# First layer's eleventh pair of steps nested, outer weight sums split between VectorE and POOL, and a transfer's room moved into finished weights

## The chip, the core and the metric

The kernel runs on one core of a Trainium2 chip. The metric is device time in microseconds, as the median of three executions: 848.37 us (848.19 to 848.67). One further execution was profiled: it took 848.57 us, and the program's span in its trace is 846.8 us, so 1.77 us of its time lie around the span. Every time below that is read from the trace belongs to that one execution, and is counted from the span's start.

## What is computed

An attention over 4 batches, 8 heads, 768 tokens and head size 64, in which a query sees only keys of the same 6-bit hash bucket, and then a two-layer network on the 3072 tokens:

```
scores = np.where(q_bucket == k_bucket, scale * q @ k.T, -1e9)
attn = softmax(scores);  x = (attn @ v) as (3072, 512)
h = x @ w_in                                 # (3072, 512) @ (512, 2048)
g = h * (1.0 / (1.0 + np.exp(-1.702 * h)))
return (g @ w_out).astype(np.float32)        # (3072, 2048) @ (2048, 512)
```

All of it is float32. The change is in the two layers of the network alone.

## The kernel before, in words

**Two layers as Strassen-like products.** Both layers use a seven-product scheme in place of eight (Winograd's form). One operand is cut into quarters `a11..a22`, and `sums_a` (lines 219 to 225) makes four sums of them, S1 to S4; the other is cut into `b11..b22`, and `sums_b` (L227 to L233) makes t1, d12, t2 and t4. The dictionaries `LEFT` and `RIGHT` say which quarter or sum each of the products 1 to 7 takes. A sum that is written `s3` stands in the place of `a21`, and `d12` in the place of `b12`.

**First layer.** The tokens come in three blocks of 1024 (`sb`), and for each block `MT` = 8 steps (`mt`) each make 128 columns of the hidden layer on either side of the cut: 24 steps, numbered n = 0 to 23. A step's seven products have two matrix instructions of 512 columns each (`product`, L895 to L900); float32 instructions appear as two records each in the trace. ScalarE applies the activation, POOL makes the second layer's outer sums of its result (`g_outer`), and each result goes to `g_dram` in device memory (`keep`, L902 to L910).

**Nested pairs.** Two steps 2t and 2t+1 can be run as one pair (`pair_of_steps`). There the products 2, 4 and 3 of the two steps together are again cut in quarters (`nest_w`, `nest_x`, `nested`, L969): seven instructions of 256 columns instead of eight, for each of the three. `NESTED` is the range of the pairs t that are run so: 1 to 9, which are the steps 2 to 19. Steps 0, 1 and 20 to 23 run through `hidden`. The pairs of even t hold their results in tiles of the pool `stage`, those of odd t in `twice`; the nested sums of weights are also in `twice`, and for t of 2 and 3 they hold a fourth tile, so that the quarter `x[2]` stays whole. A pair lays out part of its work for the other engines in `agenda`, in slots 1 to 17, of which the slots past 8 fall into the next pair or step.

**Second layer.** There are 21 outer products (`steps_out`, three token blocks times `OUTER` = 1, 2, 6, 7, 5, 3, 4), and each is again a seven-product scheme of 256 columns with four matrix instructions for each product (`product_of_halves`, L1217 to L1283, order of products 1, 2, 3, 6, 7, 5, 4). An outer product n needs three things: two transfers of 1 MB from `g_dram` (`fetch(n)`, L1176 to L1180; the first brings b11 and b12, the second b21 and b22), into one of two rooms (`raw_g[0]`, a tile of its own, for even n; `raw_g[1]`, in `s_in`, for odd n); the sums of what was fetched, by VectorE (`g_sums(n)`); and the sums inside its weights, by POOL (`inner_sums`, with places from the list `rooms`).

**The outer sums of the output weights.** The seven left operands `wqs` are four quarters of the converted `w_out_sb` and three sums over them, made by `sums_a` in two halves of columns, `low` and `high`, of four sums each. Before, all eight are VectorE's, and they are spread over steps 20 to 23 (`between` and `todo`).

**Order.** TensorE, VectorE, ScalarE and POOL run in the order in which the program gives its instructions. The queue of SyncE (SP), which issues the fetches and most of the stores, is ordered when the program is built, by the times that the builder estimates. It issues in that order, and an entry that waits holds back all entries behind it. ScalarE issues the conversion's loads and the nested pairs' direct stores on a queue of its own.

The conversion of `w_out` (lines 170 to 208, six VectorE instructions and one of ScalarE to a chunk) runs beside the first layer, the last of its 16 chunks at step 20.

Of the kernel before, what the change touches and what calls it, by code (L numbers as in the profile page):

```python
# [8 lines left out]
F32 = mybir.dt.float32  # L9
# [10 lines left out]
P = 128  # L20
# [18 lines left out]
def kernel(  # L39
# [17 lines left out]
    nc = tc.nc  # L57
# [178 lines left out]
    XT = 512  # L236
# [609 lines left out]
    def feed_forward(tag, late=()):  # L846
# [9 lines left out]
        with ExitStack() as fctx:  # L856
# [7 lines left out]
            twice_ctx = fctx.enter_context(ExitStack())  # L864
            twice = None
            MT = FC // 2
            NESTED = range(1, MT + 2)
            sets = [small_ctx.enter_context(tc.tile_pool(name=f"f1{tag}", bufs=1, space=PSUM, side="right"))]
# [14 lines left out]
            def staged_pair(name, second):  # L883

                held[name] = (twice if second else stage).tile([P, 2 * XT], F32, tag=name, name=name)
                return held[name]

            def staged(name, n):

                if n in (0, 2 * NESTED.stop) and (name, n) not in made:  # L890
                    made[name, n] = staged_pair(name, False)
                return held[name][:, n % 2 * XT : (n % 2 + 1) * XT]
# [40 lines left out]
            def nest_w(t):  # L933
                sums = {}
                m = slice(2 * t * P, (2 * t + 2) * P)
                for o in TWICE:
                    w = quarters_in(m)[LEFT[o]]
                    x = [w[:, k, i * P : (i + 1) * P] for i in range(2) for k in range(2)]
                    n = 3 if t < 2 else 4
                    new = w_out_sb[:, t - 2, 12:16, :] if (o, n) == (4, 4) else twice.tile([P, n, P], F32, name=f"w{o}{t}")  # L940
                    new = [new[:, i] for i in range(n)]
                    s3 = x[2] if n == 3 else new[3]
                    W[o, t] = [x[0], x[1], s3, x[3]] + new[0:3]
                    sums[o] = sums_a(nc.gpsimd, x[0], x[1], s3, x[3], *new[0:3], a21=x[2])
                return sums
# [57 lines left out]
            def plan(t, at, *fs, small=False):  # L1003
                agenda.setdefault(8 * t + at, ([], []))[0 if small else 1].extend(fs)
# [133 lines left out]
            def outer_sums(*args):  # L1138
                t = [x.tile([P, XT], F32, tag=f"t{i}", name=f"t{i}") for x in places_of_sums for i in (1, 2, 4)]
                for f in g_outer(*args, *(t or (args[2], args[5], args[4]))):  # L1140
                    for x in f:
# [9 lines left out]
                     for x in (xT[:, 3], s_room) for i in range(4)]  # L1151
            rooms[4:4] = [w_in_sb[:, :, F2 * i + mt * P : F2 * i + (mt + 1) * P] for mt in range(FC // 2) for i in range(2)]
            wholes = [xT[:, i, 4 * XT : 6 * XT] for i in range(4)] + [t_x[:, i].rearrange("p k t -> p (k t)") for i in range(2)]
# [18 lines left out]
            steps_out = [(sb, o) for sb in range(n1) for o in OUTER]  # L1172
            raw_g = [None, s_in[:, 0:2].rearrange("p i k f -> p (i k f)").rearrange("p (c t) -> p c t", t=XT)]

# [6 lines left out]

            g_tiles = {}

            def g_quarters(n):
                if n not in g_tiles:


                    g_tiles[n] = wholes[4:6] if n == 1 else [
                        (st2 if n % 2 else gp).tile([P, F4, TH], F32, tag=t, name=t + "ab"[n % 2]) for t in ("t1", "t2")]
                    g_tiles[n] = g_tiles[n] + [gp.tile([P, F4, TH], F32, tag="t4", name="t4g")]  # L1190
# [26 lines left out]
            def product_of_halves(n, acc, after):  # L1217
# [3 lines left out]
                m = wholes[n % len(wholes)]  # L1221
                u, v = (gp.tile([P, TH], F32, tag=x, name=x, bufs=2) for x in ("u", "v"))
                c11, c12, c21, c22 = (m[:, i] for i in range(4))
# [83 lines left out]
            twice = twice_ctx.enter_context(tc.tile_pool(name=f"tw{tag}", bufs=1, side="right"))  # L1307
            wop = fctx.enter_context(tc.tile_pool(name=f"wo{tag}", bufs=1))
            cv_ctx = fctx.enter_context(ExitStack())
# [11 lines left out]
                      for k, i in ((3, 0), (2, 0), (3, 0), (3, 1))]  # L1321
            spare += [s_in[:, 0:2, :, 0 : 2 * P], s_in[:, 2, :, 0:XT]]
# [12 lines left out]

# [13 lines left out]
            for t in NESTED:  # L1349
# [27 lines left out]
            for n in range(2 * NESTED.stop, 3 * MT):  # L1377
                sb, mt = divmod(n, MT)
                if n == 2 * NESTED.stop + 1:
                    assert not agenda  # L1380
                    inner_ctx.close()
                    twice_ctx.close()
# [12 lines left out]
            t_ctx.close()  # L1395
            stage_ctx.close()
            st2 = fctx.enter_context(tc.tile_pool(name=f"st2{tag}", bufs=1, side="right"))
# [110 lines left out]
```

## Time and profile before

| | |
|---|---|
| median of three runs | 848.37 us (848.19 to 848.67) |
| profiled execution: own time, span | 848.57 us, 846.8 us |
| TensorE busy, share of the span | 838.2 us, 99% |
| VectorE busy | 674.6 us, 80% |
| POOL busy | 366.3 us, 43% |
| ScalarE busy | 337.2 us, 40% |
| mean granted TensorE clock | 0.999 |
| attention | up to 308 us |
| first layer, TensorE | 308.44 to 586.3 us |
| second layer, TensorE | 586.3 to 840.3 us |

How to read the rows below: a row of the timeline has the start, the length (of several merged instructions, from the first start to the last end), the engine (SPq and ACTq are the queues in which SyncE and ScalarE issue transfers), the line, the operation, the tile written and the tiles read, the shape and a count; in brackets stands how long the engine was idle before, and what released it. A modelled end of a matrix instruction overlaps the next one's start, so the distance from start to start is its cost. A row of transfers gives their count, their size and the median time from issue to landing.

### The profile page before, as it was taken

The page shows a single profiled execution, that of the slowest core. Times are in us where ns is not written, and L with a number is a line of the kernel's source. Part 1 is how long each engine was busy: PE and PEld are TensorE (multiplying, and loading weights), DVE is VectorE, ACT ScalarE, POOL GpSimd, SP SyncE. Part 2 cuts the span into 40 slices and gives each one's busy share as a digit, 9 for nine tenths or more (in the row PEclk, how much of TensorE's full clock was granted, in tenths as well). Part 3 has the DMA queues.
Part 4 walks back from the last instruction along what each step waited for, and adds up shares of the span by engine and source line. Part 5 has one row for each costly group of instructions (what it writes and reads, how often), then busy time and mean ns, then how long its engine had stood idle before and what let it go on. Part 6 is the DMA issues. An engine that isn't in the chain of part 4 may idle for free.

```text
span 846.8 us, 14953 instructions
## 1 busy us (share of the span) xinstructions
PE 838.2 (99%) x5644; PEld 520.8 (62%) x5644; DVE 674.6 (80%) x1068; ACT 337.2 (40%) x552; POOL 366.3 (43%) x321
## 2 busy tenths in 40 slices
PE   9999999999999999999999999999999999999996
PEld 4544444444444444566666666545888888888885
DVE  6478888887888985788888788577998977796776
ACT  7766766767676634433444344433000000000000
POOL 5433443434344358996844486578655000000000
PEclk9999999999999999999999999999999999999999
DMA  8679766777763105445555545587754685467524
GB/s 143 120 154 167 163 131 142 146 150 148 155 156 95 49 2 174 150 158 215 216 196 198 210 174 224 198 298 257 264 192 156 195 254 192 155 201 248 194 106 101
DMA packets 165197, 144.92 MB, mean 171 GB/s; under 512 B 124224, under 2 KB 139712, under 8 KB 159872
## 3 DMA queue, kind: packets, MB, share of 16 engines
q1 hardware_dynamic: 154640, 112.11, 47.7%
q10 hardware_dynamic: 10480, 31.81, 11.3%
q8 instruction: 45, 0.74, 0.4%
q14 instruction: 32, 0.26, 0.1%
HBM read 79.69 MB, written 50.33 MB: 154 GB/s over the span
## 4 chain that ended last, share of the span: by engine, by line
PE 98%; POOL 1%; ACT 0%; issue 0%; DVE 0%; ACTq 0%; POOLq 0%
PE product L1228 30%; PE product L899 23%; PE s L547 15%; PE s L514 15%; PE small L969 6%; PE product L969 3%; PE s L496 2%; PE s L460 1%; PE s L569 1%; POOL above L339 0%; PE s L410 0%; POOL feat L337 0%; ACT c L914 0%; DVE v L917 0%; ACT size L198 0%
## 5 line engine op out<-in xcount | busy, mean ns | idle before, releaser
L484 ACT ACTIVATE e<-s 128x768 f32<-128x768 f32 x192 | 143.2, 812 | 49.2 <-PE s L514 43.9
L547 PE MATMUL s<-e,v 128*32 128x385 f32 x1536 | 130.9, 488 | 0.0
L525 POOL TENSOR_TENSOR t_x<-e 128x768 f32<-128x768 f32 x32 | 60.5, 1891 | 136.2 <-ACT e L484 126.1
L899 PE MATMUL product<-xT,w_in_sb 128*128 128x512 f32 x216 | 100.0, 593 | 0.1
L547 PEld LDWEIGHTS s<-e,v 128*32 128x32 f32 x1536 | 46.7, 109 | 79.3 <-issue 62.8
L899 PE MATMUL product<-t_x,s_in 128*128 128x512 f32 x192 | 89.5, 593 | 0.0
L514 PE MATMUL s<-s_in 32*128 32x384 f32 x912 | 87.8, 481 | 0.0
L525 POOL TENSOR_TENSOR t_x<-t_x,e 128x768 f32<-128x768 f32 x32 | 55.1, 1723 | 43.4 <-ACT e L484 42.0
L538 DVE TENSOR_TENSOR acc<-acc,e 128x768 f32<-128x768 f32 x63 | 70.1, 1113 | 2.3
L1264 ACT COPY u<-product 128x256 f32<-128x256 f32 x20 | 7.4, 372 | 158.4 <-PE product L1228 125.2
L899 PEld LDWEIGHTS product<-xT,w_in_sb 128*128 128x128 f32 x216 | 40.9, 190 | 35.8 <-issue 32.7
L514 PEld LDWEIGHTS s<-s_in 32*128 32x128 f32 x912 | 43.8, 185 | 23.4 <-issue 2.2
L899 PEld LDWEIGHTS product<-t_x,s_in 128*128 128x128 f32 x192 | 36.4, 190 | 29.9 <-issue 26.8
L514 PE MATMUL s<-own 32*128 32x384 f32 x432 | 44.3, 482 | 0.0
L465 DVE TENSOR_SCALAR f<-s,above,weight 128x384 bf16<-128x384 f32 x15 | 10.2, 678 | 39.1 <-PE s L569 33.9
L917 DVE TENSOR_TENSOR u<-product,u 128x256 f32<-128x256 f32 (+1 forms) x60 | 28.4, 486 | 15.5 <-PE product L969 12.9
L1228 PE MATMUL product<-raw_g,xT 128*128 128x256 f32 x152 | 35.1, 379 | 0.0
L535 DVE SCALAR_TENSOR_TENSOR acc<-t_x,e 128x768 f32<-128x768 f32 x31 | 29.3, 946 | 6.7 <-POOL t_x L525 3.6
L231 POOL TENSOR_TENSOR v<-c,v 128x1024 f32<-128x1024 f32 (+1 forms) x15 | 32.3, 2155 | 1.0
L230 POOL TENSOR_TENSOR u<-v,u 128x1024 f32<-128x1024 f32 (+1 forms) x11 | 23.8, 2166 | 20.6 <-ACT v L914 11.3
L917 DVE TENSOR_TENSOR v<-product,v 128x512 f32<-128x512 f32 x24 | 16.5, 689 | 20.0 <-PE product L899 20.0
L1228 PEld LDWEIGHTS product<-raw_g,xT 128*128 128x128 f32 x152 | 28.9, 190 | 3.9
(297 smaller groups left out, 1774.0 us busy)
## 6 DMA issues: line engine op xcount, KB each, us to landing
raw_g<-g_dram SPq DMA_DIRECT2D x20, 1024.0 KB, 5.1
s_in<-g_dram SPq DMA_DIRECT2D x20, 1024.0 KB, 5.0
g_dram<-c ACTq DMA_DIRECT2D x18, 512.0 KB, 2.8
raw<-in_moe_w_out_dram ACTq DMA_DIRECT2D x16, 512.0 KB, 3.7
raw<-in_moe_w_in_dram ACTq DMA_DIRECT2D x15, 512.0 KB, 3.8
s_in<-own SPq DMA_DIRECT2D x36, 192.0 KB, 4.0
v<-in_v_dram SPq DMA_DIRECT2D x16, 384.0 KB, 4.0
k<-in_k_dram SPq DMA_DIRECT2D x52, 96.0 KB, 3.0
```

Source lines behind the costliest of these rows:

```text
L230: return [lambda: eng.tensor_tensor(t1, b12, b11, op=Alu.subtract), lambda: eng.tensor_tensor(b12, b22, b12, op=Alu.subtract), lambda: eng ...
L231: lambda: eng.tensor_tensor(b12, b22, b12, op=Alu.subtract),
L484: nc.scalar.activation(es[c][:, kt, :, 0:HS], ps[:, :, 0:HS], Act.Exp, scale=1.0 / D**0.5)
L514: nc.tensor.matmul(ps[i][:, j, 0:HS], a[r0 : r0 + 32, keys], m[r0 : r0 + 32, cols], start=at == 0, stop=at == 2)
L525: nc.gpsimd.tensor_tensor(low_sum, low_sum if i else e[:, 0], e[:, i + 1], op=Alu.add)
L535: nc.vector.scalar_tensor_tensor(acc, terms[0], T * TINY, terms[1], op0=Alu.add, op1=Alu.add)
L538: nc.vector.tensor_tensor(acc, acc, terms[i + 1], op=Alu.add)
L547: nc.tensor.matmul(av[D * j + d : D * j + d + 32, :], vt[:, j, row, d : d + 32], es[c][:, t, j, :], start=(t == 0), stop=(t == T - 1))
L899: nc.tensor.matmul(ps, wq[LEFT[i]][:, kc, :], xq[RIGHT[i]][:, kc, :], start=(start and kc == 0), stop=(kc == K2 - 1), skip_group_check=not ...
L917: nc.vector.tensor_tensor(dst, x, y, op=Alu.add)
L969: nc.tensor.matmul(x, wq[LEFT[i]], xq[RIGHT[i]], start=start, stop=True, skip_group_check=True)
L1228: nc.tensor.matmul(ps, wq[LEFT[i]][:, c, :], gq[RIGHT[i]][:, c, :], start=(onto is None and c == 0), stop=(c == F4 - 1), skip_group_check= ...
```

## The change

- `NESTED` now ends with pair 10, so the steps 20 and 21 run as a nested pair too, and only 0, 1, 22 and 23 run through `hidden`. For t = 2 the nested weight sums now overwrite `x[2]`, and they have a pool of their own, `nest`.
- The eight outer sums of weights are dealt out: the four of `low` into slots 1, 5, 2, 3 of pair 10, three on POOL and one (the second) on VectorE; `high[0]` and `high[2]` on VectorE at the end of step 22 and within step 23, `high[1]` and `high[3]` on POOL behind step 23.
- `inner_sums(0)` stays at pair 9; `inner_sums(1)` is put at the end of step 22, ahead of that step's own outer sums of results, which are now written out at the start of step 23; `inner_sums(2)` comes at the end of step 23, with `g_sums(0)` in step 23 as well.
- `raw_g[0]` is no tile of its own any more but lies in the columns of `w_in_sb` that steps 0 to 3 of a token block use; `fetch(0)` stands ahead of step 22, `fetch(1)` within step 23. Eight new tiles (`more`) replace the rooms for inner sums that those columns had held.
- The tiles of `stage` are taken over for `wide` (VectorE's sums of fetched results, and the products' u and v), and `twice` stays open to the end of the first layer.

```diff
-            NESTED = range(1, MT + 2)
+            NESTED = range(1, MT + 3)
...
-                    n = 3 if t < 2 else 4
-                    new = w_out_sb[:, t - 2, 12:16, :] if (o, n) == (4, 4) else twice.tile([P, n, P], F32, name=f"w{o}{t}")
+                    n = 3 if t < 3 else 4
+                    new = w_out_sb[:, t - 2, 12:16, :] if (o, n) == (4, 4) else nest.tile([P, n, P], F32, name=f"w{o}{t}")
...
-            rooms[4:4] = [w_in_sb[:, :, F2 * i + mt * P : F2 * i + (mt + 1) * P] for mt in range(FC // 2) for i in range(2)]
+            rooms[4:4] = [w_in_sb[:, :, F2 * i + mt * P : F2 * i + (mt + 1) * P] for mt in range(4, FC // 2) for i in range(2)]
...
-            raw_g = [None, s_in[:, 0:2].rearrange("p i k f -> p (i k f)").rearrange("p (c t) -> p c t", t=XT)]
+            raw_g = [w_in_sb.rearrange("p c (i f) -> p (c i) f", i=2)[:, :, 0:XT], s_in[:, 0:2].rearrange("p i k f -> p (i k f)").rearrange("p (c t) -> p c t", t=XT)]
...
-            low, high = (sums_a(nc.vector, *(x[:, :, F4 * c : F4 * (c + 1), :] for x in wqs)) for c in range(2))
+            low, high = ([sums_a(eng, *(x[:, :, F4 * c : F4 * (c + 1), :] for x in wqs))[i] for i, eng in enumerate(engs)]
+                         for c, engs in enumerate(((nc.gpsimd, nc.vector, nc.gpsimd, nc.gpsimd),
+                                                   (nc.vector, nc.gpsimd, nc.vector, nc.gpsimd))))
             first = 2 * NESTED.stop
-            between = {first + 1: low[1:2], first + 2: high[:1], first + 3: high[2:3]}
-            todo[first] = todo.get(first, []) + low[:1]
-            todo[first + 1] = low[2:] + inner_sums(1)
-            todo[first + 2] = high[1:2]
-            todo[first + 3] = high[3:] + inner_sums(2)
+            todo[first] = high[:1] + inner_sums(1)
...
+                if t + 2 == NESTED.stop:
+                    plan(t, 5, *inner_sums(0))
                 if t + 1 == NESTED.stop:
-                    plan(t, 5, *inner_sums(0))
+                    for i, f in zip((1, 5, 2, 3), low):
+                        plan(t, i, f)
...
-                if n == 2 * NESTED.stop + 1:
+                between, end = [], []
+                if n == 2 * NESTED.stop:
+                    fetch(0)
+                else:
...
-                    raw_g[0] = gp.tile([P, FC // 2, XT], F32, name="raw_g")
+                    more = gp.tile([P, 8, F4, P], F32, name="rooms")
+                    rooms[8:8] = [more[:, i] for i in range(8)]
+                    wide += [stage.tile([P, 4, TH], F32, tag=x, name="wide") for x in ("u", "v", "c21", "c22")]
...
                     outer_sums(*heads.pop("sums"))
-                    fetch(0)
-                t = {3 * MT - 2: g_sums(0)[:1], 3 * MT - 1: g_sums(0)[1:]}.get(n, []) if n > 3 * MT - 3 else []
-                hidden(sb, mt, between.get(n, []) + ([lambda: fetch(1)] if n == 3 * MT - 1 else []), t + todo.pop(n, []))
+                    g = g_sums(0)
+                    between, end = [high[2], g[0], lambda: fetch(1)], g[1:] + inner_sums(2) + [high[1], high[3]]
+                hidden(sb, mt, between, todo.pop(n, []) + end)
```

More of the change, by code (lines that the diff above doesn't have):

```diff
@@ L865, in feed_forward @@
             twice = None
+            nest_ctx = fctx.enter_context(ExitStack())
+            nest = None
             MT = FC // 2
-            NESTED = range(1, MT + 2)
+            NESTED = range(1, MT + 3)
             sets = [small_ctx.enter_context(tc.tile_pool(name=f"f1{tag}", bufs=1, space=PSUM, side="right"))]
@@ L890, in staged @@
                 if n in (0, 2 * NESTED.stop) and (name, n) not in made:
-                    made[name, n] = staged_pair(name, False)
+                    made[name, n] = staged_pair(name, n > 0)
                 return held[name][:, n % 2 * XT : (n % 2 + 1) * XT]
@@ L1180, in fetch @@
                     loader[0].dma_start(out=raw_g[n % 2][:, cs], in_=g_dram[len(LEFT) * sb + RIGHT[o], :, cs, :])
-            g_tiles = {}
+            g_tiles, wide = {}, []
             def g_quarters(n):
@@ L1188, in g_quarters @@
                     g_tiles[n] = wholes[4:6] if n == 1 else [
-                        (st2 if n % 2 else gp).tile([P, F4, TH], F32, tag=t, name=t + "ab"[n % 2]) for t in ("t1", "t2")]
-                    g_tiles[n] = g_tiles[n] + [gp.tile([P, F4, TH], F32, tag="t4", name="t4g")]
+                        st2.tile([P, F4, TH], F32, tag=t, name=t + "b") for t in ("t1", "t2")] if n % 2 else wide[0:2]
+                    g_tiles[n] = g_tiles[n] + [wide[2]]
                 g = raw_g[n % 2]
@@ L1221, in product_of_halves @@
                 m = wholes[n % len(wholes)]
-                u, v = (gp.tile([P, TH], F32, tag=x, name=x, bufs=2) for x in ("u", "v"))
+                u, v = (wide[3][:, 2 * (n % 2) + i, :] for i in range(2))
                 c11, c12, c21, c22 = (m[:, i] for i in range(4))
@@ L1307, in feed_forward @@
             twice = twice_ctx.enter_context(tc.tile_pool(name=f"tw{tag}", bufs=1, side="right"))
+            nest = nest_ctx.enter_context(tc.tile_pool(name=f"ne{tag}", bufs=1, side="right"))
             wop = fctx.enter_context(tc.tile_pool(name=f"wo{tag}", bufs=1))
@@ L1321, in feed_forward @@
                       for k, i in ((3, 0), (2, 0), (3, 0), (3, 1))]
-            spare += [s_in[:, 0:2, :, 0 : 2 * P], s_in[:, 2, :, 0:XT]]
+            spare += [s_in[:, 0:2, :, 0 : 2 * P], s_in[:, 2, :, 0:XT], s_in[:, 0:2, :, 2 * P : 4 * P]]
             steps = conversions(cv, cps, late + chunks)
@@ L1378, in feed_forward @@
                 sb, mt = divmod(n, MT)
-                if n == 2 * NESTED.stop + 1:
+                between, end = [], []
+                if n == 2 * NESTED.stop:
+                    fetch(0)
+                else:
                     assert not agenda
                     inner_ctx.close()
-                    twice_ctx.close()
+                    nest_ctx.close()
                     cv_ctx.close()
@@ L1390, in feed_forward @@
                     outer_sums(*heads.pop("sums"))
-                    fetch(0)
-                t = {3 * MT - 2: g_sums(0)[:1], 3 * MT - 1: g_sums(0)[1:]}.get(n, []) if n > 3 * MT - 3 else []
-                hidden(sb, mt, between.get(n, []) + ([lambda: fetch(1)] if n == 3 * MT - 1 else []), t + todo.pop(n, []))
+                    g = g_sums(0)
+                    between, end = [high[2], g[0], lambda: fetch(1)], g[1:] + inner_sums(2) + [high[1], high[3]]
+                hidden(sb, mt, between, todo.pop(n, []) + end)
                 yield
             t_ctx.close()
-            stage_ctx.close()
+            twice_ctx.close()
             st2 = fctx.enter_context(tc.tile_pool(name=f"st2{tag}", bufs=1, side="right"))
```

## The prediction

> **What bounds the kernel now.** I read the page first, then the chain of waits around the change (549 to 600 us), then TensorE's timeline there, and after that the timelines of the engines and queues that feed it. The page:
>
> ```profile
> span 846.8 us, 14953 instructions
> PE 98%; POOL 1%; ACT 0%; issue 0%; DVE 0%; ACTq 0%; POOLq 0%
> ```
>
> TensorE is the chain. So the change can gain only by taking work or waits from TensorE, and lose only by making it wait. The chain around the steps that are changed:
>
> ```profile
> 552.63 1.05 ACT c L914
> 553.70 0.33 ACTq L909
> 554.08 0.65 ACT size L198
> 554.72 0.52 ACT v L1097
> 555.28 31.17 PE product L899 x72
> ```
>
> Here TensorE waits once, for ScalarE's copy v, which stands behind an activation, a store and a conversion's instruction (L198). Behind that the chain shows no wait. TensorE's own rows, one for each landmark:
>
> ```profile
> 512.47 1.88 PE L899 MATMUL product<-xT,w_in_sb 128*128 128x512 f32 x4
> ...
> 535.27 1.88 PE L899 MATMUL product<-t_x,s_in 128*128 128x512 f32 x4
> ...
> 551.60 3.60 PE L899 MATMUL product<-t_x,s_in 128*128 128x512 f32 x8
> 555.28 5.42 PE L899 MATMUL product<-xT,w_in_sb 128*128 128x512 f32 x12
> ...
> 567.40 5.31 PE L899 MATMUL product<-xT,w_in_sb 128*128 128x512 f32 x12
> ...
> 579.42 3.60 PE L899 MATMUL product<-xT,w_in_sb 128*128 128x512 f32 x8
> ...
> 586.29 3.62 PE L1228 MATMUL product<-raw_g,w_out_sb 128*128 128x256 f32 x16
> ...
> 598.37 3.62 PE L1228 MATMUL product<-s_in,w_out_sb 128*128 128x256 f32 x16
> ```
>
> The second layer starts at 586.29. Its outer product n=1, which reads s_in, starts at 598.37, 12.08 later, so a single product of n=1 takes 12.08 / 7 = 1.73.
>
> **What TensorE saves.** A nested pair has the same records at the same places 22.80 us apart (512.47 to 535.27). A plain step takes 12.02 (567.40 to 579.42), two of them 24.04. Nesting steps 20 and 21 saves 24.04 - 22.80 = 1.24 us. The wait at 555.28: eight records at 12.02 / 28 = 0.429 from 551.60 end at 555.03, so 0.25 was idle; the 28 records from 555.28 to 567.40 took 12.12, another 0.10. The conversion's last chunk moves into the pair, so L198 (0.65) no longer stands ahead of copy v, which then comes before it is needed: a gain of 0.35. Together -1.59. The pair's slots then run 22.80 later than the rows of pair 9, and the second layer starts at 584.7, its product n=1 at 596.8 and the second product of n=1 at 598.5, if nothing is late.
>
> **Edits that I cost at nothing.** The three low sums on POOL (three rows of 128x1024) fall behind pair 9's stretch, before POOL waits for an activation; the VectorE sum in slot 5 takes the place of conversion instructions that are no longer in that half of the pair. If that cover were gone, a VectorE sum would cost its 1.2 to 2.3. fetch(0) goes out about 25 us ahead of its use, in runs of 2 KB instead of 8 KB; even the slowest landing below, 9.9, hides behind that. The g sums of n=0 are nearer: in the queue worked out below, d12 ends at about 590.9 and product 7 needs it at 591.6.
>
> **The transfer that is late.** In the built program, SyncE's queue of the changed kernel reads, from the last nested pair on: store s_in (pair 10's fourth sum), stores t1, v, t2, t4 (step 22's outer sums by POOL), stores c22 and u of step 23, then both halves of fetch(1), then the store c21. Before, the first half of fetch(1) went out ahead of those stores and the second behind the last t. These rows show it:
>
> ```profile
> 577.90 0.32 SPq L1180 DMA_DIRECT2D s_in<-g_dram  x1
> ...
> 583.72 2.63 SPq L909 DMA_DIRECT2D g_dram<-t  x2
> 586.44 0.38 SPq L909 DMA_DIRECT2D g_dram<-c  x1
> 586.92 0.41 SPq L909 DMA_DIRECT2D g_dram<-u  x1
> 587.42 0.40 SPq L1180 DMA_DIRECT2D s_in<-g_dram  x1
> ...
> 596.51 0.37 SPq L1180 DMA_DIRECT2D raw_g<-g_dram  x1
> ...
> 596.98 0.41 SPq L1180 DMA_DIRECT2D raw_g<-g_dram  x1
> ```
>
> So in the changed kernel nothing of fetch(1) can go out before POOL has made the last outer sum of step 22. On POOL that sum is now behind the pair's fourth sum, the four of `inner_sums(1)` and three outer sums. POOL's rows before:
>
> ```profile
> 553.82 2.37 POOL L233 TENSOR_TENSOR s_in<-c,c 128x1024 f32<-128x1024 f32 x1 [4.15 <-ACT c L914]
> ...
> 574.21 1.26 POOL L223 TENSOR_TENSOR w_out_sb<-w_out_sb 128x512 f32<-128x512 f32 x1
> 575.43 1.27 POOL L224 TENSOR_TENSOR w_in_sb<-w_in_sb,w_out_sb 128x512 f32<-128x512 f32 x1
> 576.77 1.27 POOL L225 TENSOR_TENSOR w_in_sb<-w_out_sb,w_in_sb 128x512 f32<-128x512 f32 x1
> 578.00 2.25 POOL L230 TENSOR_TENSOR t<-v,u 128x512 f32<-128x512 f32 x1
> 580.33 2.13 POOL L231 TENSOR_TENSOR v<-c,v 128x512 f32<-128x512 f32 x1
> 582.42 1.28 POOL L232 TENSOR_TENSOR t<-c,t 128x512 f32<-128x512 f32 x1
> 583.77 2.23 POOL L233 TENSOR_TENSOR t<-c,t 128x512 f32<-128x512 f32 x1
> ```
>
> ```profile
> 576.80 2.33 DVE L230 TENSOR_TENSOR t1a<-raw_g 128x1024 f32<-128x1024 f32 x1
> 579.05 2.28 DVE L223 TENSOR_TENSOR w_out_sb<-w_out_sb 128x1024 f32<-128x1024 f32 x1
> ...
> 583.66 1.21 DVE L224 TENSOR_TENSOR xT<-xT,w_out_sb 128x1024 f32<-128x1024 f32 x1
> ```
>
> Alone, a POOL sum of 512 goes every 1.27 (574.21 to 578.00, three). Against VectorE's sums over 1024 both run in turn: POOL's go from 578.00 to 580.33 to 582.42, 2.2 each, while VectorE's stretch from 1.21 to 2.3.
>
> The sum: pair 10's fourth POOL sum stands where 553.82 stood, 22.80 later, at 576.62, for it waits for an activation of the pair; it ends at 579.0. Eight sums of 512 follow. VectorE is then done with `high[0]` and waits for step 23's products, so three of the eight run alone: 579.0 + 3 x 1.27 = 582.8. From there VectorE has five sums over 1024 (`high[2]`, t1, t2, d12, t4 of n=0), one against each of the five left: 582.8 + 5 x 2.25 = 594.1. Bounds: all eight alone 589.2, all eight in turn 597.0.
>
> Then SyncE: before, the last t ended on POOL at 583.77 + 2.23 = 586.0, and the transfer behind stores t, c and u went out at 587.42, 1.42 later. So 595.5 for the first half, and the second 0.47 behind (596.51 to 596.98), at 596.0. How long such transfers take:
>
> ```profile
> raw_g<-g_dram SPq DMA_DIRECT2D x1, 1024.0 KB, 6.4
> raw_g<-g_dram SPq DMA_DIRECT2D x1, 1024.0 KB, 9.9
> s_in<-g_dram SPq DMA_DIRECT2D x1, 1024.0 KB, 6.1
> s_in<-g_dram SPq DMA_DIRECT2D x1, 1024.0 KB, 7.0
> ```
>
> The first two are the pair issued at 596.51 and 596.98, back to back as fetch(1) would be; the third is that of 587.42, with stores ahead of it; the fourth one that overlaps the end of another. I take 6.4 and 9.9, the pair being the nearest case: the halves land at 601.9 and 605.9. Product 1 of n=1 wants the first at 596.8 and waits 5.1; product 2 could then start at 603.6 and waits 2.3 more. TensorE stands 605.9 - 598.5 = 7.4 us longer than it would. Bounds: 589.2 + 1.89 + 7.0 = 598.1, no wait, and 597.0 + 1.89 + 9.9 = 608.8, 10.3.
>
> Queued behind the late halves are VectorE's sums of n=1 (t1 waits for the first, t2 for the second) and, on SyncE, step 23's stores and fetch(2). Product 6 of n=1 needs t2 two products after the second half, 3.45 us, and a sum in turn takes 2.3, so that is covered; fetch(2), at about 601, has until 616.
>
> The whole: 848.57 - 1.59 + 7.4 = 854.4 on the profiled execution's scale. The median of the runs stands 0.2 below that execution, so 854.2.
>
> **The rivals.**
>
> A. The transfer is hidden after all. POOL runs its eight sums alone or nearly so and the halves land in 7: the low bounds give no wait, so 848.57 - 1.59 - 0.2 = 846.8, faster than before by 0.19%. Speaking for it: SyncE waits at no place of TensorE's chain now, and the start of n=1 is 12 us behind that of the layer. Against: VectorE must make its five sums in just that stretch, since TensorE reads t2, d12 and t4 there, and each costs POOL about 1.0. It decides at a landing of the second half by 598.5.
>
> B. The wait costs more than itself. POOL's two `high` sums over 1024 (rows as 553.82: 2.4 each) come at about 607 to 611, when VectorE makes d12 of n=1, due at 610.8: up to 2.4 late. Or the clock drops in the wait:
>
> ```profile
> 844.30:845.30 1.00, 0.00 (x0) 0.00 (x0) 0.00 (x0) 0.00 (x0) 0.00 (x0) 1.00 0.10 25
> 845.30:846.30 1.00, 0.00 (x0) 0.00 (x0) 0.00 (x0) 0.00 (x0) 0.00 (x0) 0.68 0.00 0
> ```
>
> (The columns are the stretch, its length, five engines, the granted clock, then transfers.) After TensorE's last instruction, which ends at 840.3 (586.45 and the 253.83 us of the chain's last row below), the clock is whole until 845.3; 0.68 over the next microsecond, if it goes to half, places the drop 0.64 before that stretch's end, at 845.7, after 5.4 us idle. A first wait of 5.1 stays just short; a longer one would run the eight records of product 1 and then part of product 2 at half speed, of which the wait for the second half hides the first: about 1.7. So 856 to 857.
>
> ```profile
> 586.45 253.83 PE product L1228 x1176
> ```
>
> The Trainium skill, "TensorE: Matmul & The Clock Gate", part 1 on the HAM clock gate, has the array at half clock after one idle window of about 3.4 us that runs free of the kernel. By that page a wait of 5.1 would more often than not meet such a window; the row above held out longer, and by the row the sum has no such term.
>
> C. The change doesn't do what it says: pair 10 waits inside for nested sums of weights that now overwrite their source, and gives its 1.24 back. Pairs 4 and 8, 5 and 9 already read such sums in place, and the trace shows pairs at 22.80; if so, 855.4.
>
> **How the numbers follow.** The forecast has 0.74 (its own range 850.5 to 856.5, from POOL ending between 591 and 596), A 0.12, B 0.12, C 0.02. The range for eight in ten reaches from 850.3, where POOL is half helped and the halves land sooner, to 857, where B lies. A difference under 0.2%, 1.7 us, cannot be told from none: 846.67 to 850.07. A sits at the lower edge of that, so faster by more has 0.03; within has 0.12 (the rest of A and the forecast's shortest waits); slower by more has 0.85.
>
> **What would show it.** Right: TensorE starts the second layer near 584.7, then stands twice, before the first and the second product that read s_in, and the releaser is the transfer; SyncE's two s_in issues come back to back near 595.5, right behind stores of t, c and u; POOL's t4 of step 22 ends near 594. Pairs 1 to 10 are 22.80 apart and copy v is no longer awaited at step 23. Wrong: s_in issued before 590, or TensorE without a gap behind 584; a gap at n=0 waiting for VectorE instead would be the sums and not the transfer.

## The result, and the profile after

| | before | after |
|---|---|---|
| median of the runs, side by side | 848.39 us (848.19 to 848.98) | 855.29 us (854.43 to 855.83) |
| ratio, 95% interval | 1 | 1.0079 (1.0066 to 1.0092) |
| span of the profiled execution | 846.8 us | 853.6 us |

The change makes the kernel slower by 6.9 us. The page of the kernel after, its first line and the shares of the chain that ended last:

```profile
span 853.6 us, 14973 instructions
PE 94%; POOL 3%; DVE 1%; DMA 1%; issue 1%; ACT 0%; SPq 0%; POOLq 0%; DVEq 0%
```

TensorE held 98% of that chain before and holds 94% now; POOL's share has gone from 1% to 3%. The chain of waits of the kernel after, with the rows from pair 10 to the second layer's second outer product:

```profile
535.33 1.72 PE product L901 x4
...
558.12 1.72 PE product L901 x4
...
572.31 1.73 PE product L901 x4
574.06 0.70 DVE v L919
575.32 1.05 ACT c L916
576.51 2.35 POOL s_in L233
...
591.57 2.14 POOL t L233
595.45 6.27 DMA s_in<-g_dram
...
605.03 3.37 DVE t_x L232
608.99 2.71 DVE s_in L231
611.74 28.33 PE product L1230 x130
```

Read from top to bottom, it leaves TensorE at 574.06 and comes back at 611.74: an activation of pair 10, POOL's fourth sum of the pair, the eight POOL sums behind it (the last is shown), the transfer, then VectorE's sums of n=1. The two records at 535.33 and 558.12 stand 22.79 us apart: pair 10 costs what the other pairs cost. SyncE's queue of the kernel after:

```profile
591.52 2.53 SPq L911 DMA_DIRECT2D g_dram<-t  x2
594.16 0.36 SPq L911 DMA_DIRECT2D g_dram<-c  x1
594.63 0.40 SPq L911 DMA_DIRECT2D g_dram<-u  x1
595.45 0.81 SPq L1182 DMA_DIRECT2D s_in<-g_dram  x2
```

The second of the two stores of t goes out when POOL's sum of 591.57 has ended, at 593.7; c and u, long finished, stand behind it, and fetch(1) behind them. Before, the first half of fetch(1) went out at 577.90. What that does to TensorE, in its timeline after (a bracket is idle time and its releaser):

```profile
584.59 3.62 PE L1230 MATMUL product<-w_in_sb,w_out_sb 128*128 128x256 f32 x16
...
594.95 1.89 PE L1230 MATMUL product<-wide,w_out_sb 128*128 128x256 f32 x8
601.86 5.59 PE L1230 MATMUL product<-s_in,w_out_sb 128*128 128x256 f32 x16 [5.01 <-DMA s_in<-g_dram]
607.28 1.89 PE L1230 MATMUL product<-s_in,w_in_sb 128*128 128x256 f32 x8
609.01 1.89 PE L1230 MATMUL product<-t_x,w_in_sb 128*128 128x256 f32 x8
611.74 1.99 PE L1230 MATMUL product<-s_in,w_out_sb 128*128 128x256 f32 x8 [0.84 <-DVE s_in L231]
613.57 1.89 PE L1230 MATMUL product<-t_x,w_in_sb 128*128 128x256 f32 x8
...
617.03 3.62 PE L1230 MATMUL product<-w_in_sb,xT 128*128 128x256 f32 x16
```

The layer starts at 584.59 against 586.29, 1.70 sooner. Product 1 of n=1 was due at 594.95 + 1.73 = 596.68 and starts at 601.86, 5.18 late. Products 1 and 2 take 607.28 - 601.86 = 5.42 where 3.45 is their cost, 1.97 more. Product 7 starts 2.73 after product 6 where 1.73 is due, 1.00 more, and itself takes 0.10 more. That is 8.25, less 1.70 makes 6.55; n=2 starts at 617.03 against 610.46, 6.57 later, and nothing is lost behind it: the last product starts at 844.95 against 838.38.

Product 7 waits for d12, which VectorE makes behind t2. The chain above has t2 at 3.37 (605.03) and d12 at 2.71 (608.99), where a VectorE sum of this size takes 1.21 alone. POOL's two sums over 1024 run beside them:

```profile
604.79 2.52 POOL L223 TENSOR_TENSOR w_out_sb<-w_out_sb 128x1024 f32<-128x1024 f32 x1
607.28 3.32 POOL L225 TENSOR_TENSOR xT<-w_out_sb,xT 128x1024 f32<-128x1024 f32 x1
```

### The profile page after: what moved, and what is told of

Its sections match the earlier page's. It is cut to its first block, busy times and chain, and to the rows that moved or that the text cites. A ratio compares the mean times of both kernels' runs of the same rounds, so it can differ in the third digit from the quotient of the medians.

```text
span 853.6 us, 14973 instructions
## 1 busy us (share of the span) xinstructions
PE 838.7 (98%) x5662; PEld 524.9 (61%) x5662; DVE 673.9 (79%) x1079; ACT 337.3 (40%) x550; POOL 372.3 (44%) x322
## 4 chain that ended last, share of the span: by engine, by line
PE 94%; POOL 3%; DVE 1%; DMA 1%; issue 1%; ACT 0%; SPq 0%; POOLq 0%; DVEq 0%
PE product L1230 28%; PE product L901 21%; PE s L547 15%; PE s L514 15%; PE small L971 7%; PE product L971 4%; PE s L496 2%; PE s L460 1%; PE s L569 1%; DMA s_in<-g_dram 1%; DVE t_x L232 0%; DVE s_in L231 0%; POOL s_in L233 0%; POOL t L230 0%; POOL t L232 0%
## 5 line engine op out<-in xcount | busy, mean ns | idle before, releaser
L901 PE MATMUL product<-xT,w_in_sb 128*128 128x512 f32 x208 | 96.8, 592 | 0.0
L1266 ACT COPY wide<-product 128x256 f32<-128x256 f32 x20 | 7.4, 371 | 165.9 <-PE product L1230 132.7
L1230 PE MATMUL product<-s_in,w_out_sb 128*128 128x256 f32 x136 | 33.2, 397 | 5.9 <-DMA s_in<-g_dram 5.0
L230 POOL TENSOR_TENSOR u<-v,u 128x1024 f32<-128x1024 f32 (+1 forms) x12 | 26.2, 2182 | 21.4 <-ACT v L916 12.4
L1230 PE MATMUL product<-w_in_sb,xT 128*128 128x256 f32 x152 | 35.1, 379 | 0.0
L919 DVE TENSOR_TENSOR c<-small,c 128x256 f32<-128x256 f32 (+1 forms) x60 | 26.8, 460 | 9.2 <-PE small L971 9.1
L1230 PEld LDWEIGHTS product<-s_in,w_out_sb 128*128 128x128 f32 x136 | 27.1, 200 | 10.5 <-POOL xT L223 5.4
```

The costliest lines, as they stand in the source:

```text
L230: return [lambda: eng.tensor_tensor(t1, b12, b11, op=Alu.subtract), lambda: eng.tensor_tensor(b12, b22, b12, op=Alu.subtract), lambda: eng ...
L901: nc.tensor.matmul(ps, wq[LEFT[i]][:, kc, :], xq[RIGHT[i]][:, kc, :], start=(start and kc == 0), stop=(kc == K2 - 1), skip_group_check=not ...
L919: nc.vector.tensor_tensor(dst, x, y, op=Alu.add)
L1230: nc.tensor.matmul(ps, wq[LEFT[i]][:, c, :], gq[RIGHT[i]][:, c, :], start=(onto is None and c == 0), stop=(c == F4 - 1), skip_group_check= ...
```

## The experiments

Each run was timed beside the kernel before on the same chip, and its ratio is to that. "Waits" are TensorE's between 584 and 640 us in the profiled execution.

| run | what differs | median, before | ratio (95%) | waits |
|---|---|---|---|---|
| e5 | before, fetch(1) behind the stores | 848.54, 848.71 | 0.9996 (0.9987 to 1.0006) | none |
| e1 | changed, fetch(1) ahead of the stores | 851.16, 849.05 | 1.0021 (1.0013 to 1.0030) | t2 of n=2, 1.9 |
| e2 | changed, POOL's outer sums first | 851.01, 849.05 | 1.0024 (1.0014 to 1.0034) | fetch(2), 2.9 |
| e4 | changed, fetch(1) on ScalarE's queue | 851.78, 849.05 | 1.0029 (1.0018 to 1.0040) | t2 of n=2, 2.0 |
| e6 | changed, high sums by VectorE | 854.69, 848.71 | 1.0069 (1.0053 to 1.0084) | fetch(1), 4.6 |
| e7 | e1 and high sums by VectorE | 850.54, 848.71 | 1.0023 (1.0014 to 1.0032) | fetch(2), 2.3 |
| e8 | e7 and half of fetch(2) early | 849.28, 848.71 | 1.0006 (0.9997 to 1.0015) | fetch(2), 1.5 |
| e9 | e7 and both halves of fetch(2) early | 847.83, 848.55 | 0.9990 (0.9981 to 0.9999) | none |
| e10 | e9, high sums left on POOL | 851.83, 848.55 | 1.0033 (1.0019 to 1.0046) | t2 of n=2, 2.2 |
| e3 | changed, idle matrix work in the wait | 854.16, 849.05 | 1.0058 (1.0037 to 1.0079) | behind that work: fetch(1), 0.7 |
| e11 | the changed kernel again | 855.83, 849.13 | 1.0070 (1.0056 to 1.0084) | fetch(1), 5.3; d12, 0.7 |
| e12 | e3 again | 853.70, 849.13 | 1.0067 (1.0053 to 1.0081) | behind that work: product 2, 0.5 |

**e1: fetch(1) ahead of the stores that wait for POOL.** The two halves are issued before any of the four stores of step 22's sums: `behind_issue(x, y)` puts x behind y in a queue's order and waits for nothing.

```diff
...
-                    outer_sums(*heads.pop("sums"))
+                    def fetch_first():
+                        dma, count = fetch(1), len(stored)
+                        outer_sums(*heads.pop("sums"))
+                        for store in stored[count:]:
+                            behind_issue(store, dma)
...
-                    between, end = [high[2], g[0], lambda: fetch(1)], ...
+                    between, end = [high[2], g[0], fetch_first], ...
```

> The changed kernel with one order turned round: the two halves of fetch(1) are put ahead of the four stores of step 22's outer sums in SyncE's queue (and, with them, ahead of the stores c22 and u of step 23 where the builder's times allow). POOL's sums, the transfer's size and its room stay. Theory Q (the transfer was late only because it stood behind stores that wait for POOL): the first half goes out by about 583-585, when the store of pair 10's fourth sum has landed, both halves land before 596.8, TensorE waits for no transfer behind 584.6, and the time is 848.4 - 1.6 = 846.8. Rival D (the transfer itself is slow, in its new neighbourhood of rooms and loads): sent out early it still lands late or slows the others, and at least half of the loss stays, 851 or more. Rival S (the sums are the bound: POOL and VectorE in turn): the transfer is early but TensorE waits for VectorE at n=0 or n=1 instead, about 848-850.

SyncE's queue in e1:

```profile
581.95 0.32 SPq L1182 DMA_DIRECT2D s_in<-g_dram  x1
...
583.27 0.82 SPq L1182 DMA_DIRECT2D s_in<-g_dram  x1
...
599.68 2.53 SPq L911 DMA_DIRECT2D g_dram<-t  x2
602.31 0.98 SPq L1182 DMA_DIRECT2D w_in_sb<-g_dram  x2
```

Both halves go out 13 us sooner, with POOL's sums and the room untouched, and TensorE waits for fetch(1) no more: product 1 of n=1 starts at 596.79. So the queue's order made the transfer late, and rival D's reason is out. But the time is 851.2 and not the 846.8 of theory Q; it is D's figure (851 or more), for another reason. The last row shows a second transfer in the same place: fetch(2), 602.31, stands behind the last t of step 23. It lands only just in time here (products 1 and 2 of n=2 take 3.77 instead of 3.45), and TensorE waits 1.9 us for VectorE's t2 of n=2 instead, at half clock for some products behind it.

**e2 and e4: the same by other means.** In e2 `outer_sums` is called ahead of `inner_sums(1)`, with the queue's order as it was; in e4 fetch(1) alone is issued by ScalarE.

```diff
-            todo[first] = high[:1] + inner_sums(1)
+            todo[first] = high[:1]
...
                     outer_sums(*heads.pop("sums"))
+                    for f in inner_sums(1):
+                        f()
```

```diff
-                    loader[0].dma_start(out=raw_g[n % 2][:, cs], ...
+                    (nc.scalar if n == 1 else loader[0]).dma_start(out=raw_g[n % 2][:, cs], ...
```

> The changed kernel with POOL's order turned round: step 22's four outer sums stand ahead of the four of inner_sums(1). SyncE's queue stays as it was, with fetch(1) behind the stores of the outer sums. Theory Q: those sums end about 4 x 1.35 = 5.4 us sooner, near 588.3, so fetch(1) goes out at about 589.5-590, its halves land at about 595.8 and 599.5-600, and TensorE, which wants the second at 598.4, waits 1 to 1.6: 848 to 848.4, that is, the same as before. Rivals D and S: moving POOL's sums about without changing their number leaves the time at 855 (D) or moves the wait to the inner sums of n=1 (S), 851 or more.

> The changed kernel with fetch(1) alone issued on ScalarE's queue instead of SyncE's; all waits of the transfer on its data stay. Theory Q: it goes out at about 583, lands by 593, and the time is 846.8, as with the stores put behind it; ScalarE loses two issues (about 0.5 each), which its idle time hides. Rival D: no gain, 853 or more, since the transfer is the same. Rival S: the wait moves to VectorE's sums, 848-850.

In both fetch(1) is early (issued from 585.39 and from 582.72) and its wait is gone; both stop near 851. For e2 the expectation had POOL's outer sums ending at 588.3; three of the four ran alone and the last ended at 584.9, so that fetch(1) was not late at all. What came next it missed; TensorE's timeline of e2:

```profile
611.91 3.72 PE L1230 MATMUL product<-w_in_sb,xT 128*128 128x256 f32 x16 [2.94 <-DMA w_in_sb<-g_dram]
```

fetch(2) again. In e4 it is t2 again. Three ways of making fetch(1) early give the same two new waits, so these belong to the changed kernel and not to an edit. All three missed the time that theory Q gave. Rival S, by which the sums of the two engines are the bound, named a wait for VectorE such as e1 and e4 show; e9 below decides on it.

**e5: the order alone, in the kernel before.**

```diff
...
+                    for store in stored[-6:] if n == 1 else ():
+                        behind_issue(dma, store)
```

> The kernel before, with one order alone taken over from the change: both halves of fetch(1) are put behind the stores of step 22's outer sums and behind c22 and u of step 23. POOL's queue stays short there (its last outer sum of step 22 ends at 586.0). Theory Q (the order in the queue costs only as much as POOL is late): both halves go out at 587.4 to 588, land at about 594 and 598, product 1 wants the first at 598.4 and product 2 the second at 600.1: no wait, a ratio of 1.000 to before. Rival O (standing behind the stores is itself the loss): the wait appears here too, 2 us or more, 850.5 and up.

Both halves went out from 587.29 on, behind the stores, and took 6.2 and 8.3; no wait followed, and rival O is out. The second had landed by about 596.2, in time even for the changed kernel's 596.68. Standing behind the stores cost nothing with POOL done by 586; it is the four inner sums that the change puts ahead of them that make it late, as e2 shows from the other side. Order and load are a cause only together.

**e6: the two high sums by VectorE.**

```diff
-                                                   (nc.vector, nc.gpsimd, nc.vector, nc.gpsimd))))
+                                                   (nc.vector, nc.vector, nc.vector, nc.vector))))
```

> The changed kernel with high[1] and high[3] made by VectorE instead of POOL, behind its sums of n=0, where it stands idle until the transfer lands. SyncE's order and the late fetch(1) stay. Theory Q: only the last part of the bill goes, the 0.84 that TensorE waits for d12 of n=1, so 854.4 (ratio 1.007). Rival P (POOL's sums over 1024, in turn with VectorE, are the main cost, and the late transfer only uncovers them): 852 or less.

The wait for d12 is gone and the one for fetch(1) stays, at 4.6. In the trace n=2 starts 31.86 after the layer (616.82 - 584.96) where it was 32.44: undone alone, this link is worth 0.6, less than the intervals can tell, and rival P is out. The sum behind it is mixed: product 1 starts 4.78 late instead of 5.18, the 1.10 at product 7 is gone, but products 1 and 2 take 6.36 (601.83 to 608.19) instead of 5.42, since the granted clock fell later here and stayed at half until 607.6.

**e7 to e10: the links together.** e7 is e1 with e6, where high[1] goes right behind high[0]. e8 and e9 add this for fetch(2), e8 for the second half alone, e9 for both; e10 is e9 without the edit of e6.

```diff
-                    fetch(n + 1)
+                    halves = fetch(n + 1)
+                    for store in stored[-4:] if n == 1 else ():
+                        for dma in halves:
+                            behind_issue(store, dma)
```

> The order of e1 (fetch(1) ahead of the stores of step 22's outer sums) and high[1] and high[3] by VectorE, the first right behind high[0], where VectorE stands idle for 4 us, the second behind the sums of n=0. In e1 TensorE waited 1.9 us for VectorE's t2 of n=2, which POOL's two sums over 1024 had held up, and half clock followed. Theory L (the loss is a chain of three links: fetch(1), fetch(2), VectorE's sums against POOL's; undoing one uncovers the next): that wait goes, and the time falls from a ratio of 1.002 to between 0.998 and 1.001, the upper end if fetch(2), which still stands behind the stores of step 23, lands late as in e2 (2.9). Rival S (the work of the two sum engines is simply too much, wherever it stands): VectorE is late elsewhere and the ratio stays at 1.002 or above.

> As e7, and the first half of fetch(2) ahead of the stores of step 23's outer sums as well; it goes out when its room is free, at about 594, instead of 602.3. Theory L: no wait for a transfer and none for VectorE is left between 584.6 and 640, n=3 starts 1.6 us sooner than before (620.9 against 622.5), and the time is 846.8 where before is 848.4, a ratio of 0.998. Rival S: a ratio of 1.000 or above, with TensorE waiting for VectorE.

> As e8, but with both halves of fetch(2) ahead of the stores of step 23's outer sums: in e8 only the second had gone ahead, and TensorE waited 1.5 us for the first, which went out at 604.4, behind the last of those stores. Theory L (a chain of three links): both go out at about 597, land by 607, TensorE waits for nothing between 584.6 and 640, and the time is 1.6 us under before, a ratio of 0.998 (0.997 to 0.999). Rival S (VectorE and POOL have too much to do for the start of the second layer, so a wait for a sum comes instead): 1.000 or above, TensorE waiting for t2 or d12 of n=2.

> As e9, but with high[1] and high[3] left on POOL, where the change put them. Theory L: with both transfers early the third link alone is left: VectorE's drains and t2 of n=2 in turn with POOL's two sums over 1024, as in e1, where TensorE waited 1.9 us for t2 and half clock could follow (up to 1.8 more). So 1.9 to 3.7 above e9, a ratio of 1.000 to 1.002. Rival F (the two late transfers are all there is, and VectorE was late in e1 only because fetch(2) came late to it): the same as e9, 0.998.

e7 ended above what theory L had given: t2 was in time, but both halves of fetch(2) were late. They went out at 604.83, 2.5 later than in e1. Of that, 0.7 stands there already when POOL's fourth sum of pair 10 starts (577.31 against 576.62). Another 0.8 comes from VectorE's high[1], which now stands beside that sum (3.17 where it was 2.35), and 1.0 from one more POOL sum that then meets a VectorE sum (2.25 where it was 1.28). e8 missed theory L's 0.998 too: the half that its edit put ahead was the second and not, as the expectation has it, the first; TensorE waited 1.5 for the first, which went out at 604.39 and took 6.4. Both times lie where rival S had them, but the waits are for a transfer and not, as S has it, for VectorE. In e9 nothing is late up to 640, though the two engines make the same sums, and rival S is out as the cause of these waits. TensorE's timeline of e9, the first rows of n=0 to n=3, and a row of n=6:

```profile
584.96 3.62 PE L1232 MATMUL product<-w_in_sb,w_out_sb 128*128 128x256 f32 x16
...
597.04 3.62 PE L1232 MATMUL product<-s_in,w_out_sb 128*128 128x256 f32 x16
...
609.13 3.62 PE L1232 MATMUL product<-w_in_sb,xT 128*128 128x256 f32 x16
...
621.22 3.62 PE L1232 MATMUL product<-s_in,w_out_sb 128*128 128x256 f32 x16
...
663.00 1.97 PE L1232 MATMUL product<-wide,s_in 128*128 128x256 f32 x8 [0.18 <-DVE wide L232]
```

The outer products follow each other at 12.08 and 12.09, as before. n=3 starts 1.33 sooner than before (621.22 against 622.55). Some 0.4 is lost again by the end (621.22 to the last product's start at 837.47, against 622.55 to 838.38), of which the last row shows a part: VectorE's t2 of n=6 is late. The ratio is 0.9990 with an interval from 0.9981 to 0.9999: this version is clearly faster than the changed kernel, and faster than before by a margin that the interval only just keeps clear of none. The medians differ by 0.7 us where 1.6 was expected, and the interval holds both.

e10 puts a price on the third link. VectorE and then POOL in e10:

```profile
607.71 3.97 DVE L1237 TENSOR_TENSOR xT<-xT 128x256 f32<-128x256 f32 x2
611.61 2.57 DVE L1237 TENSOR_TENSOR xT<-xT,wide 128x256 f32<-128x256 f32 x1
614.10 1.21 DVE L230 TENSOR_TENSOR wide<-w_in_sb 128x1024 f32<-128x1024 f32 x1
...
615.90 1.21 DVE L232 TENSOR_TENSOR wide<-w_in_sb,wide 128x1024 f32<-128x1024 f32 x1
```

```profile
608.87 2.52 POOL L223 TENSOR_TENSOR w_out_sb<-w_out_sb 128x1024 f32<-128x1024 f32 x1
611.36 2.53 POOL L225 TENSOR_TENSOR xT<-w_out_sb,xT 128x1024 f32<-128x1024 f32 x1
```

and the same additions, with t2 behind them, in e9:

```profile
607.76 2.89 DVE L1237 TENSOR_TENSOR xT<-xT 128x256 f32<-128x256 f32 x2
610.58 0.41 DVE L1237 TENSOR_TENSOR xT<-xT,wide 128x256 f32<-128x256 f32 x1
...
612.71 1.21 DVE L232 TENSOR_TENSOR wide<-w_in_sb,wide 128x1024 f32<-128x1024 f32 x1
```

An addition of 128x256 takes 0.41 by itself and 2.57 where a POOL sum over 1024 has started just ahead of it (611.36 to 613.89). (In e9 the pair at 607.76 is stretched too, by POOL's shorter sums over 512.) What that does to TensorE in e10:

```profile
585.49 3.62 PE L1232 MATMUL product<-w_in_sb,w_out_sb 128*128 128x256 f32 x16
...
617.25 2.45 PE L1232 MATMUL product<-wide,rooms 128*128 128x256 f32 x8 [2.24 <-DVE wide L232]
619.49 3.14 PE L1232 MATMUL product<-w_in_sb,xT 128*128 128x256 f32 x8
```

t2 starts 30.41 after the layer (615.90 - 585.49) where it is 27.75 in e9 (612.71 - 584.96). TensorE waits 2.24 for it, and the next product takes 2.98 instead of 1.73, at half clock. The time is 851.83 against 847.83: 4.0 us from two sums in the wrong place, a little above the 1.9 to 3.7 that theory L gave. Rival F is out. The Trainium skill, "SBUF — State Buffer", section "SBUF: two separate sides", has the port pair that VectorE and POOL share as an exclusive lock for a whole instruction, which a VectorE operation with two inputs in SBUF needs as well. These rows agree: the addition of 611.61 ends at 614.18, right behind POOL's sum.

**e3, e11, e12: what the clock costs.** In the changed kernel, 44 matrix instructions on idle data are added in TensorE's wait.

```diff
+                    for _ in range(44 if (n, i) == (1, 1) else 0):
+                        nc.tensor.matmul(ps, idle[:, 0:P], idle[:, 0:TH], start=True, stop=True)
```

> The changed kernel, with 44 matrix instructions on idle data (128x256, bfloat16, about 4.7 us together) put into TensorE's wait ahead of product 1 of n=1; the bank is overwritten by the product, so only the clock is touched. Rival C (the drop of the clock is what the wait costs beyond itself): the granted clock stays at 1.0 between 598 and 607, products 1 and 2 take 3.45 of TensorE's time instead of 5.4, and the time falls by about 2, to 853.3. Theory Q with its own sizes: product 1 at full clock ends at 603.6 and then waits for the second half until 605.0, product 2 ends at 606.7 instead of 607.3, and the wait for d12 (VectorE, 611.7) takes up what was won: 854.7 to 855.3, within 0.5 of the changed kernel.

> The changed kernel itself, beside the next run on one chip, so that the two can be told apart by less than a microsecond. Every theory: 6.9 us over before, a ratio of 1.008; TensorE waits about 5 us for fetch(1) and the granted clock falls to half in the wait.

> The kernel of e3 once more (the changed kernel with 44 matrix instructions on idle data in TensorE's wait), with more rounds and beside the changed kernel on the same chip, since e3's interval (1.0037 to 1.0079) holds both answers. Theory Q with its own sizes (the second half of the transfer and VectorE's d12 hide most of what the clock costs): 0 to 0.6 us under the changed kernel. Rival C (the clock is what the wait costs beyond itself): 1.7 to 2.3 under it.

The granted clock around the wait, in the kernel after (stretch, length, the busy time of five engines, clock, transfers):

```profile
596.00:598.00 2.00, 0.84 (x4) 0.39 (x3) 0.00 (x0) 0.00 (x0) 1.92 (x3) 1.00 1.09 307
598.00:600.00 2.00, 0.00 (x0) 0.00 (x0) 0.00 (x0) 0.00 (x0) 2.00 (x2) 0.72 0.94 238
...
602.00:604.00 2.00, 2.00 (x5) 1.65 (x6) 2.00 (x2) 0.00 (x0) 1.92 (x2) 0.50 0.97 386
604.00:606.00 2.00, 2.00 (x7) 1.59 (x7) 1.90 (x4) 0.35 (x1) 2.00 (x2) 0.57 1.07 391
```

A mean of 0.72 between whole and half puts the drop at 598.9, 2.2 us after TensorE's last product was through (596.68), and it is whole again at 605.7. So product 1 ran at half clock. The transfers of fetch(1) in the kernel after, least, median and most from issue to landing:

```profile
DMA to landing us min/median/max: 6.3/7.3/8.4
```

The second half, issued at about 595.85, had landed by 604.3, before product 1 at half speed was through at 605.3: the 1.97 in products 1 and 2 is the clock, and no second wait. At whole clock product 1 ends at 603.6 and product 2 waits 0.7, so the clock itself costs about 1.3 by estimate. In e3 and e12, where it stayed at 1.00, products 1 and 2 took 4.41 and 4.20 (601.70 to 605.90), against 5.42 in the kernel after and 5.29 in e11: 1.0 and 1.1 less. The n=2 of e12 starts 30.13 after the layer (614.94 - 584.81) against 32.46 in e11 (617.71 - 585.25), and e3 and the kernel after show 30.14 and 32.44; the rest of these 2.3 is an earlier start of product 1 (0.4 and 0.7) and a shorter wait for d12 (by 0.9 and 0.6), since t2 got its turn ahead of POOL's long sum. So neither expectation held in full: the traces gain what rival C gave (1.7 to 2.3), but only half of it in products 1 and 2, where theory Q's wait for the second half came back. The timed runs of e11 and e12 overlap, however (853.5 to 856.3 and 853.4 to 856.0), and so do their intervals. The clock's share is read from two pairs of traces, and no run shows it in the time.

## Why the prediction was right, and where it was not

- **What TensorE saves** (1.24 for the pair, 0.35 for copy v, a start at 584.7): measured 584.59, and no wait at step 23. Right; of the 1.70, 0.11 stood there ahead of pair 10 already (a record ahead of both pairs, at 512.47 before, is at 512.36 after). Rival C fell with the 22.79.
- **POOL's queue** (start 576.62, end 594.1, five of eight sums in turn): start 576.51, end 593.70, five sums between 2.12 and 2.25 and three at 1.27. Right.
- **SyncE** (issue at 595.5 and 0.47 behind, right behind t, c and u): 595.45. Right, and e1, e2 and e5 show it as a cause that needs both the order and the load.
- **The first wait** (6.4 to land, TensorE 5.1 late): 6.27 and 5.18. Right.
- **The second wait** (9.9 to land, 2.3 more): the mechanism was wrong, and that the size came out nearly right is luck. The half landed in 8.4, which leaves 0.7 of waiting; half clock took its place, with 1.97 in all. The step that failed is "a first wait of 5.1 stays just short": it was sized by the one idle stretch of the trace before, at the kernel's end, where the clock held for 5.4 us. In the kernel after it fell 2.2 us into the wait. The rule that the prediction set against that row (the Trainium skill, "TensorE: Matmul & The Clock Gate", part 1: half clock after an idle window of about 3.4 us) pointed the right way, but a fall after 2.2 us is sooner than a whole idle window allows. Nor would a wait of 5.1 meet a whole window of 3.4 "more often than not": wherever the windows lie, that is an estimate of 1.7 in 3.4, one case in two.
- **VectorE behind the late halves** ("that is covered"): t2 was in time, but t2 and d12 were stretched to 3.37 and 2.71 by POOL's two sums over 1024, so that d12 came 1.00 late. Rival B had this with 2.4 as its bound, and the forecast left it out of its sum. With 5.18, 1.97, 1.00 and 0.10 the bill is 8.25 where 7.4 was forecast, and the time 855.3 where 854.2 was. The first of the four, and what makes it, is what the forecast had right.
- **Rival A** (846.8 once the transfer is hidden) had a wrong price. e1 hid it, with a landing well before 598.5, and stopped at 851.2. The prediction gave fetch(2) until 616, which holds only when n=1 is itself late; without that wait it has until 608.9, goes out at 602.3 and takes 6 to 9, and VectorE is held up as well. The first wait had covered two more: of the 6.9 us, e1 won 4.8 (2.1 over before instead of 6.9). All three have to be undone, as in e9, for the nested pair's gain to show.

## What to carry to other kernels

In a queue that issues in order, look at what every entry ahead of an urgent transfer waits for: a store that waits for a slow engine turns that engine's load into a delay of the transfer, and each of the two alone may cost nothing. When the slack of the next transfer or sum is read off a trace, work it out for the kernel without the wait too, since a long wait hides the shorter ones behind it. Long sums of one engine are best kept out of the stretch where the other has short, urgent additions over the same memory.

## What the runs showed of the hardware

The clock's fall follows no fixed length of idle time. It came 2.2 us into the wait of the kernel after, where it had held for 5.4 us at the end of the kernel before (0.68 between 845.3 and 846.3). In e1 a wait of 1.9 us was followed by it, when TensorE was at work again, and in e2 one of 2.9 us was not. The granted clock in e1 (the columns as above):

```profile
614.00:615.00 1.00, 0.54 (x3) 0.13 (x1) 1.00 (x3) 0.37 (x1) 0.00 (x0) 1.00 0.65 270
615.00:616.00 1.00, 0.00 (x0) 0.00 (x0) 1.00 (x2) 0.00 (x0) 0.00 (x0) 1.00 0.00 0
616.00:617.00 1.00, 0.53 (x3) 0.51 (x4) 1.00 (x2) 0.00 (x0) 0.61 (x1) 1.00 0.00 0
617.00:618.00 1.00, 1.00 (x4) 0.82 (x3) 1.00 (x3) 0.00 (x0) 1.00 (x2) 0.52 0.00 0
...
620.00:621.00 1.00, 1.00 (x5) 0.85 (x4) 0.96 (x2) 0.00 (x0) 1.00 (x2) 0.78 0.11 14
```

TensorE (the first of the busy times) has done nothing between 614.5 and 616.5 and is busy again when the clock goes to half, at about 617. Worked out in the same way from the mean clock of each stretch, the length of the half clock comes in two sizes: 3.4 us in e1 (617.0 to 620.4) and e10 (618.6 to 622.0), and 6.8 us in the kernel after (598.9 to 605.7), e11 (599.5 to 606.4) and e6 (600.7 to 607.6). The Trainium skill, "TensorE: Matmul & The Clock Gate", part 1, has the clock follow windows of about 3.4 us that run free of the kernel. That the place of the fall varies agrees with it, and so do the two lengths, once and twice 3.4. That a wait of 1.9 us sufficed in e1, and 2.2 us in the kernel after, does not, if a whole idle window is needed; the traces decide, and by them a window that is idle in part can be enough.
